# A second x tile transposed by DMA instead of on TensorE, in the opening of a linear-attention and token-MLP kernel

## The chip, the cores and the metric

The kernel runs on one core of a Trainium2 chip. The core has a matrix engine (TensorE, PE in the profile; its weight loads are listed as PEld), a vector engine (VectorE, DVE), a scalar engine (ScalarE, ACT), GpSimd (POOL), SyncE (SP), which here only issues DMA transfers, and 16 DMA engines that serve all queues. The metric is the device time of one execution in microseconds, as the median of several runs.

## The reference

Two branches read the same input x of 2048 rows (s) by 512 columns (d) and are mixed by a gate per row:

```
a = linear_attention(x)      # q,k,v = x @ wqkv, 32 heads of 16
    pq, pk = phi(q), phi(k)              # phi(t) = (t+1 if t>0 else exp(t)) + 1e-6
    kv = pk^T v ; z = sum over s of pk   # per head
    o = (pq kv) / (pq z + 1e-6) ; a = o @ wo
b = token_mlp(x)             # mixes along s, not along d
    h = layernorm(x)
    u = gelu(h^T @ w1 + b1)              # w1: 2048 x 1792
    b = (u @ w2 + b2)^T                  # w2: 1792 x 2048
g = sigmoid(sum over d of x * gate_w)
out = g * a + (1 - g) * b
```

All inputs are in bf16.

## The kernel before, in words

The 2048 rows are 16 tiles of 128 rows. Two copies of x are kept on chip: `xs` in its natural layout (row on the partition) and `xT` with the columns on the partition. k = x Wk needs `xT` as weights and `wk_sb` (Wk, four chunks of 128 x 512) as the moving operand. The kernel writes the order of all work by hand: every engine runs its instructions in the order in which the program lists them.

**The opening.** SP and ACT both issue loads. SP loads x tile 0 (L136), x tile 1 (L138) and Wk chunk 3 (L140) as plain transfers, and then tiles 2, 3 and 4 straight into `xT`, each by a DMA transpose of its own (L141, L142, issued by `load_xT`, L131). Behind them SP goes on, from L157 on, with a transpose of tiles 5 and 6 together, plain x tiles 2 and 3, a transpose of tiles 7 to 9, plain x tiles 4 to 7, a transpose of 10 to 12, plain tiles 8 to 15, a transpose of 13 to 15, and then wq, w1, wv and wo. ACT issues Wk chunks 0 and 1 in one transfer (L137) and chunk 2 (L139), and then loads its function table (L189).

**Tiles 0 and 1** are not transposed by DMA. TensorE multiplies each 128 x 128 block of `xs` by an identity matrix (`transpose_part`, L194, into PSUM tiles `pt`), and DVE or ACT copies the result to `xT` (`copy_part`, L199). While TensorE has no data it runs six matmuls of 128 x 512 on constants (`warm_up`, L184 and L190, tile `wps`).

**The k loop.** For tile t, `k_part` issues four matmuls into one PSUM bank `kacc`, and `k_phi` turns the bank into `pk` (ACT: exp; DVE: min/add and max/add). From t = 4 on, `g_tile(t-4)` adds four matmuls `gacc` with `xs` tile t-4 as weights and `pk` tile t-4 as moving operand. So TensorE alternates: k of tile 4, g of tile 0, k of tile 5, g of tile 1, and so on. The first two tiles (`HEADS = 2`, L281 to L293) have an order of their own, in which the chunks of k of tiles 0 and 1 are interleaved with the transposes of tile 1, and the layernorm statistics (`ln_step`) of both come before the loop. In the loop, `ln_step(t-5)` starts with t = 7.

**Later stages**, which the change leaves alone: q blocks together with the first three blocks of the MLP's first product (`uacc`, L404), the rest of that product (L443), and one loop over output tiles (L482) with attention output (`aps`) and the MLP's second product (`yps`). `load_w2` (L432) brings each of four column chunks of w2 in two transfers, issued in the third stage.

Transfers issued by SP and ACT share eight completion semaphores in turn. A transfer that takes a semaphore again waits until the eighth transfer before it has landed.

Of the kernel before, what the change touches and what calls it, by code (L numbers as in the profile page):

```python
# [15 lines left out]
def kernel(  # L16
# [13 lines left out]
    nc = tc.nc  # L30
# [10 lines left out]
    ND = D // P  # L41
    NF = F // P
    SC = 512
# [25 lines left out]
    def bank(name, dtype=FP32):  # L69
        return ps.tile([P, SC], dtype, name=name, tag="bank")  # L70
# [38 lines left out]
    def mm(o, lhsT, rhs, start, stop, **kw):  # L109
        nc.tensor.matmul(o, lhsT=lhsT, rhs=rhs, start=start, stop=stop, **kw)  # L110
# [14 lines left out]
    def load_x(q, t0, n):  # L125
        q.dma_start(out=xs[:, t0 : t0 + n, :], in_=x_view[:, t0 : t0 + n, :])

    def load_wk(q, k, n):
        q.dma_start(out=wk_sb[:, k : k + n, :], in_=wqkv_view[:, k : k + n, D : 2 * D])

    def load_xT(t0, n):  # L131
        nc.sync.dma_start(
            out=xT[:, :, t0 * P : (t0 + n) * P], in_=X[t0 * P : (t0 + n) * P, :], transpose=True
        )

    load_x(nc.sync, 0, 1)  # L136
    load_wk(nc.scalar, 0, 2)  # L137
    load_x(nc.sync, 1, 1)  # L138
    load_wk(nc.scalar, 2, 1)  # L139
    load_wk(nc.sync, 3, 1)  # L140
    for t in (2, 3, 4):  # L141
        load_xT(t, 1)  # L142
    nc.vector.memset(ones_f[:], 1.0)
    nc.vector.memset(mhalf[:], -0.5)
    nc.gpsimd.memset(ident[:], 0.0)
# [29 lines left out]
    def load_small():  # L175
        nc.gpsimd.dma_start(out=brow[0:NF, :], in_=B_b1.rearrange("(f q) -> f q", q=P))
        nc.gpsimd.dma_start(out=brow[NF : NF + NT, :], in_=B_b2.rearrange("(f q) -> f q", q=P))
        nc.gpsimd.dma_start(
            out=gw_b[:], in_=gate_w.rearrange("(o d) -> o d", o=1).to_broadcast([P, D])
        )  # L180
# [3 lines left out]
    def warm_up(n, cols=SC):  # L184
        for _ in range(n):
            mm(wps[:, :cols], warm[:, 0:P], warm[:, :cols], True, True)

    act_warm = keep([P, 1], FP32, "act_warm")
    nc.scalar.activation(out=act_warm[:], in_=ones_f[:], func=ACT.Exp)  # L189
    warm_up(6)  # L190

    pts = {}

    def transpose_part(t, k0, k1):  # L194
        pt = pts[t, k0, k1] = bank("pt")
        for k in range(k0, k1):
            mm(pt[:, k * P : (k + 1) * P], xs[:, t, k * P : (k + 1) * P], ident[:], True, True)

    def copy_part(t, k0, k1, on_act):  # L199
        src = pts.pop((t, k0, k1))[:, k0 * P : k1 * P].rearrange("p (k s) -> p k s", k=k1 - k0)  # L200
        dst = xT[:, k0:k1, t * P : (t + 1) * P]
        if on_act:
            nc.scalar.activation(out=dst, in_=src, func=ACT.Copy)
        else:
            nc.vector.tensor_copy(out=dst, in_=src)  # L205

    def phi(dst, acc):
        e = work.tile([P, SC], BF16, name="e", tag="e", bufs=6)
        nc.scalar.activation(out=e[:], in_=acc[:], func=ACT.Exp)  # L209
        nc.vector.tensor_scalar(  # L210
            out=e[:], in0=e[:], scalar1=1.0, scalar2=PHI_EPS, op0=ALU.min, op1=ALU.add
        )
        nc.vector.scalar_tensor_tensor(  # L213
            out=dst, in0=acc[:], scalar=0.0, in1=e[:], op0=ALU.max, op1=ALU.add
        )
# [3 lines left out]
    def k_part(t, ks):  # L219
        if t not in kaccs:  # L220
            kaccs[t] = bank("kacc")
        for k in ks:
            mm(
                kaccs[t][:], xT[:, k, t * P : (t + 1) * P], wk_sb[:, k, :],
                k == 0, k == ND - 1,
            )

    def k_phi(t):
        phi(pk[:, t, :], kaccs.pop(t))

    def ln_stats(t):
        stats = work.tile([P, nc.vector.BN_STATS_DIM], FP32, name="stats", tag="stats", bufs=2)
        nc.vector.bn_stats(out=stats[:], in_=xs[:, t, :])  # L233
        nc.vector.bn_aggr(out=mv[:, t, :], in_=stats[:])  # L234

    def ln_rstd(g):
        s = slice(g * TPC, (g + 1) * TPC)
        nc.vector.tensor_scalar_add(out=veps[:, s], in0=mv[:, s, 1], scalar1=EPS)
        nc.gpsimd.tensor_tensor(out=rstd[:, s], in0=veps[:, s], in1=mhalf[:], op=ALU.pow)

    def ln_shift(g):
        s = slice(g * TPC, (g + 1) * TPC)
        nc.vector.scalar_tensor_tensor(  # L243
            out=nmr[:, s], in0=mv[:, s, 0], scalar=-1.0, in1=rstd[:, s],
            op0=ALU.mult, op1=ALU.mult,
        )

    def ln_apply(t):
        nc.scalar.activation(  # L249
            out=hs[:, t, :], in_=xs[:, t, :], func=ACT.Identity,  # L250
            scale=rstd[:, t : t + 1], bias=nmr[:, t : t + 1],
        )
# [3 lines left out]
    def g_tile(t):  # L256
        if not gacc:
            gacc.extend(bank("gacc") for _ in range(ND))
        for k in range(ND):
            mm(gacc[k][:], xs[:, t, k * P : (k + 1) * P], pk[:, t, :], t == 0, t == NT - 1)  # L260
# [15 lines left out]
    def ln_step(u):  # L276
        ln_stats(u)
        if u % TPC == TPC - 1:
            ln_rstd(u // TPC)

    HEADS = 2  # L281
    for t in range(HEADS):
        for k0, k1 in ((0, 1), (1, 2), (2, ND)):
            transpose_part(t, k0, k1)
            copy_part(t, k0, k1, (t, k0) in ((0, 2), (1, 1)))
        k_part(0, range(2) if t == 0 else (2,))
    k_part(1, range(2))
    k_part(0, (3,))
    k_phi(0)
    k_part(1, range(2, ND))  # L290
    k_phi(1)
    ln_step(0)
    ln_step(1)  # L293
    LAG = 4
    LN_LAG = 5
    APPLY = 10
    for t in range(HEADS, NT):
        k_part(t, range(ND))
        k_phi(t)
        if t >= LAG:  # L300
            g_tile(t - LAG)
        if t > LN_LAG + 1:
            ln_step(t - LN_LAG)
        if t == TPC - 1 + LN_LAG:
            load_small()
        if t >= APPLY:
            ln_apply(t - APPLY)
        if t in (TPC + LN_LAG, 2 * TPC + LN_LAG):
            ln_shift((t - LN_LAG) // TPC - 1)
# [122 lines left out]
    def load_w2(c):  # L432
        w = wpool.tile([P, NT, FB * P], BF16, name="w2c", tag="wc")
        w2c.append(w)
        for f0 in (0, NF // 2):
            f1 = f0 + NF // 2
            nc.sync.dma_start(
                out=w[:, f0:f1, :], in_=w2_view[:, f0:f1, c * SC : (c + 1) * SC]
            )
# [3 lines left out]
    for j in range(NB0, NF):  # L443
        c, jj = divmod(j, FB)
        i = j - NB0
        acc = bank("uacc")
        for t in range(NT):
            if i == 2 and t < BRIDGE:
                for q in range(0, P, Q32):
                    c0 = jj * P + q  # L450
                    mm(
                        acc[q : q + Q32, :], w1c[c][:, t, c0 : c0 + Q32], hs[:, t, :],
                        t == 0, False, tile_position=(0, q),
                    )
                if t == BRIDGE - 1:
                    w2_matmuls()
                continue
            mm(acc[:], w1c[c][:, t, jj * P : (jj + 1) * P], hs[:, t, :], t == 0, t == NT - 1)
        gelu(j, acc)
        if i == 1:  # L460
            kv_matmuls()
            z_column()
        if 2 <= i < 2 + ND:
            w2_copies(i - 2)
        if 2 <= i < 2 + NDB:
            den_block(*divmod(i - 2, ND))
        if 2 <= i < 2 + NT // 2:
            gate_sum(2 * i - 4)
            gate_sum(2 * i - 3)
        if jj == FB - 1 or j == NF - 1:  # L470
            load_w2(c)
# [10 lines left out]
    for t in range(NT):  # L482
        c, tl = divmod(t, TPC)
# [54 lines left out]
```

## Time and profile before

| | |
|---|---|
| median of 3 runs | 163.08 us (162.43 to 163.41) |
| the profiled execution, own time | 162.26 us |
| its span in the trace | 160.6 us |
| TensorE busy | 155.9 us (97%), 822 matmuls recorded, 836 weight loads |
| VectorE busy | 124.3 us (77%) |
| ScalarE busy | 72.7 us (45%) |
| mean DMA rate | 144 GB/s |

Times in the trace start with the span. The span leaves out what lies around the program, 162.26 - 160.6 = 1.7 us here. A matmul of 128 x 512 is listed with 379 ns, but one starts every 216 ns when nothing waits, since matmuls overlap; so busy time is a count of "has something in it", and the start times tell the rate. A few matmul records are missing (822 against 836), and each leaves an idle hole of some 53 ns in the busy time though TensorE worked there. For a DMA the trace has three things: the stretch in which its queue issues it, the packets on the DMA engines, and the time from the start of the issue to the landing.

### The profile page before, as it was taken

The numbers are of one execution on the slowest core, as the hardware profiler recorded it, in microseconds if no ns is written. First come the engines' busy times: TensorE is split into PE (matmuls) and PEld (weight loads), VectorE is DVE, ScalarE is ACT, GpSimd is POOL, SyncE is SP. The second block draws the span as 40 slices with busy tenths as digits, with TensorE's granted clock in tenths as the row PEclk, the third lists the DMA queues.
The fourth block names the chain that finished last, engine by engine and source line by source line (L and its number), as shares of the span: only waits on it lengthen the run. The fifth ranks groups of instructions, "written<-read, shape, count | busy, mean of one in ns | idle before, by whom it ended". The sixth has DMA issues, their size and how long they took to land.

```text
span 160.6 us, 2228 instructions
## 1 busy us (share of the span) xinstructions
PE 155.9 (97%) x822; PEld 72.5 (45%) x836; DVE 124.3 (77%) x274; ACT 72.7 (45%) x113; POOL 7.3 (5%) x17
## 2 busy tenths in 40 slices
PE   7999999999999999999999999999999999999993
PEld 2444444444444445444444444444444444444462
DVE  1599999769999998756999999676999999711122
ACT  3543486654978393059873320237333442111110
POOL 3000332002010000000000000000000000000000
PEclk9999999999999999999999999999999999999999
DMA  5699999999970007600930679401000001110001
GB/s 168 150 231 262 328 352 329 354 349 348 336 171 0 0 0 257 204 0 4 356 101 2 213 244 306 151 33 37 33 33 33 33 33 58 48 61 33 33 33 33
DMA packets 29929, 23.07 MB, mean 144 GB/s; under 512 B 8384, under 2 KB 29888, under 8 KB 29920
## 3 DMA queue, kind: packets, MB, share of 16 engines
q1 hardware_dynamic: 29104, 22.15, 45.2%
q10 hardware_dynamic: 704, 0.66, 1.2%
q0 software_dynamic: 112, 0.14, 0.4%
q8 instruction: 6, 0.10, 0.3%
q14 instruction: 3, 0.02, 0.0%
HBM read 19.01 MB, written 2.10 MB: 131 GB/s over the span
## 4 chain that ended last, share of the span: by engine, by line
PE 84%; DVE 13%; issue 1%; ACT 0%
PE yps L110 30%; PE uacc L110 24%; PE kacc L110 9%; PE gacc L110 9%; PE aps L110 9%; DVE pqT L213 6%; DVE zacc L274 3%; DVE stats L233 2%; DVE e L210 2%; PE wps L110 2%; PE qacc L110 1%; DVE mv L234 1%; ACT e L209 0%; PE kvps L110 0%; PE w2ps L110 0%
## 5 line engine op out<-in xcount | busy, mean ns | idle before, releaser
L110 PE MATMUL uacc<-hs,w1c 128*128 128x512 bf16 (+1 forms) x227 | 50.8, 379 | 0.4 <-issue 0.2
L110 PE MATMUL yps<-uT,w2c 128*128 128x512 bf16 (+2 forms) x247 | 50.8, 355 | 0.3
L110 PEld LDWEIGHTS <-w2c 128*128 128x128 bf16 x252 | 23.6, 98 | 25.2
L110 PEld LDWEIGHTS <-w1c 128*128 128x128 bf16 (+1 forms) x233 | 21.8, 98 | 26.0 <-issue 0.2
L488 ACT ACTIVATE a_sc<-aps,c,gg 128x512 f32<-128x512 f32 x16 | 12.4, 775 | 31.2 <-PE aps L110 15.5
L501 DVE SCALAR_TENSOR_TENSOR ot<-yps,c,a_sc 128x512 bf16<-128x512 f32 (+2 forms) x18 | 12.3, 688 | 15.3 <-PE yps L110 11.7
L322 ACT ACTIVATE uT<-uacc,bcol 128x512 bf16<-128x512 f32 x14 | 9.3, 686 | 17.5 <-PE uacc L110 17.4
L110 PE MATMUL qacc<-xT,wq_sb 128*128 128x512 bf16 x64 | 16.4, 379 | 0.1
L110 PE MATMUL aps<-W2sb,pqT 128*128 128x512 bf16 x63 | 16.4, 379 | 0.1
L110 PE MATMUL kacc<-wk_sb,xT 128*128 128x512 bf16 x63 | 15.9, 379 | 0.2 <-DVE xT L205 0.2
L387 DVE STREAM_TRANSPOSE zT<-pz 128x512 f32<-128x512 f32 x16 | 11.3, 705 | 6.0 <-ACT pz L386 6.0
L110 PE MATMUL gacc<-pk,xs 128*128 128x512 bf16 x63 | 15.7, 379 | 0.1
L249 ACT ACTIVATE hs<-xs,nmr,rstd 128x512 bf16<-128x512 bf16 x16 | 12.8, 805 | 2.3 <-DVE nmr L243 2.3
L209 ACT ACTIVATE e<-kacc 128x512 bf16<-128x512 f32 x16 | 9.4, 594 | 9.7 <-PE kacc L110 8.5
L386 ACT ACTIVATE pz<-pqT,zcol 128x512 f32<-128x512 bf16 x16 | 11.4, 715 | 4.8 <-DVE ot L501 4.7
L209 ACT ACTIVATE e<-qacc 128x512 bf16<-128x512 f32 x16 | 9.5, 594 | 7.7 <-PE qacc L110 7.7
L396 DVE STREAM_TRANSPOSE rex<-rd 128x512 bf16<-128x512 bf16 x16 | 11.4, 711 | 0.6
L213 DVE SCALAR_TENSOR_TENSOR pqT<-qacc,e 128x512 bf16<-128x512 f32 x16 | 11.1, 692 | 0.6
L213 DVE SCALAR_TENSOR_TENSOR pk<-kacc,e 128x512 bf16<-128x512 f32 x16 | 11.1, 692 | 0.6
L389 DVE TENSOR_REDUCE den<-zT 128x32 f32<-128x512 f32 x16 | 11.0, 686 | 0.6
L210 DVE TENSOR_SCALAR e<-e 128x512 bf16<-128x512 bf16 x32 | 9.0, 282 | 2.5 <-ACT e L209 2.5
L233 DVE BATCH_NORM_STATS2 stats<-xs 128x6 f32<-128x512 bf16 x16 | 10.9, 683 | 0.0
(58 smaller groups left out, 96.2 us busy)
## 6 DMA issues: line engine op xcount, KB each, us to landing
w2c<-in_B_w_dram SPq DMA_DIRECT2D x8, 896.0 KB, 5.7
w1c<-in_B_w_dram SPq DMA_DIRECT2D x3, 2048.0 KB, 14.0
out_dram<-ot SPq DMA_DIRECT2D x13, 128.0 KB, 1.7
xs<-in_A_x_dram SPq DMA_DIRECT2D x1, 1024.0 KB, 6.6
w1c<-in_B_w_dram SPq DMA_DIRECT2D x1, 1024.0 KB, 15.3
xs<-in_A_x_dram SPq DMA_DIRECT2D x1, 512.0 KB, 5.0
wq_sb<-in_A_wqkv_dram SPq DMA_DIRECT2D x1, 512.0 KB, 5.6
wv_sb<-in_A_wqkv_dram SPq DMA_DIRECT2D x1, 512.0 KB, 12.3
```

Of the source, the lines that this page charges most:

```text
L110: nc.tensor.matmul(o, lhsT=lhsT, rhs=rhs, start=start, stop=stop, **kw)
L209: nc.scalar.activation(out=e[:], in_=acc[:], func=ACT.Exp)
L210: nc.vector.tensor_scalar(out=e[:], in0=e[:], scalar1=1.0, scalar2=PHI_EPS, op0=ALU.min, op1=ALU.add)
L213: nc.vector.scalar_tensor_tensor(out=dst, in0=acc[:], scalar=0.0, in1=e[:], op0=ALU.max, op1=ALU.add)
L233: nc.vector.bn_stats(out=stats[:], in_=xs[:, t, :])
L249: nc.scalar.activation(out=hs[:, t, :], in_=xs[:, t, :], func=ACT.Identity, scale=rstd[:, t : t + 1], bias=nmr[:, t : t + 1],)
L386: nc.scalar.activation(out=pz[:], in_=seg, func=ACT.Copy, scale=zcol[:, j : j + 1])
L387: nc.vector.transpose(out=zT[:], in_=pz[:])
L389: nc.vector.tensor_reduce(out=den[:], in_=zT[:].rearrange("p (a d) -> p a d", d=HEAD), op=ALU.add, axis=AX.X)
L396: nc.vector.transpose(out=rex[:].rearrange("p (a d) -> p a d", d=HEAD), in_=rd[:].unsqueeze(2).to_broadcast([P, SC // HEAD, HEAD]),)
L488: nc.scalar.activation(out=a_sc[:], in_=aps[:], func=ACT.Identity, scale=gg[:, t : t + 1], bias=c2[:, t : t + 1],)
L501: nc.vector.scalar_tensor_tensor(out=ot[:, :W], in0=yps[:, :W], scalar=c1[:, t : t + 1], in1=a_sc[:, cs], op0=ALU.mult, op1=ALU.add,)
```

## The change

Tile 1 of x is no longer transposed on TensorE. SP issues a DMA transpose for it right behind the plain load of tile 0, and the plain load of tile 1 moves behind the transposes of tiles 1 to 4. All of Wk is issued by ACT, in three transfers: chunk 0, chunk 1, and chunks 2 and 3 together. The sixth warm-up matmul has 256 columns instead of 512. `HEADS` is 1: only tile 0 has its TensorE transposes and copies, its four k matmuls follow in one go, and tile 1 is the first of the loop. `ln_step(1)` moves from before the loop to t = 6. The first chunk of w2 comes in one transfer instead of two.

```diff
     load_x(nc.sync, 0, 1)
-    load_wk(nc.scalar, 0, 2)
+    load_wk(nc.scalar, 0, 1)
+    load_wk(nc.scalar, 1, 1)
+    load_wk(nc.scalar, 2, 2)
+    for t in (1, 2, 3, 4):
+        load_xT(t, 1)
     load_x(nc.sync, 1, 1)
-    load_wk(nc.scalar, 2, 1)
-    load_wk(nc.sync, 3, 1)
-    for t in (2, 3, 4):
-        load_xT(t, 1)
...
-    warm_up(6)
+    warm_up(5)
+    warm_up(1, SC // 2)
...
-    HEADS = 2
-    for t in range(HEADS):
-        for k0, k1 in ((0, 1), (1, 2), (2, ND)):
-            transpose_part(t, k0, k1)
-            copy_part(t, k0, k1, (t, k0) in ((0, 2), (1, 1)))
-        k_part(0, range(2) if t == 0 else (2,))
-    k_part(1, range(2))
-    k_part(0, (3,))
+    HEADS = 1
+    for k0, k1 in ((0, 1), (1, 2), (2, ND)):
+        transpose_part(0, k0, k1)
+        copy_part(0, k0, k1, k0 == 2)
+    k_part(0, range(ND))
     k_phi(0)
-    k_part(1, range(2, ND))
-    k_phi(1)
     ln_step(0)
-    ln_step(1)
...
-        if t > LN_LAG + 1:
+        if t > LN_LAG:
             ln_step(t - LN_LAG)
...
-        for f0 in (0, NF // 2):
-            f1 = f0 + NF // 2
+        n = NF if c == 0 else NF // 2
+        for f0 in range(0, NF, n):
+            f1 = f0 + n
```

## The prediction

> **What bounds the kernel now.** I read the page first, then the busy time by stretches, then the opening on SP and TensorE instruction by instruction, with each DMA's time to landing.
>
> The page, and the busy time by stretches (columns: length of the stretch, PE busy and count, clock, DMA share, GB/s):
>
> ```profile
> span 160.6 us, 2228 instructions
> PE 155.9 (97%) x822; PEld 72.5 (45%) x836; DVE 124.3 (77%) x274; ACT 72.7 (45%) x113; POOL 7.3 (5%) x17
> PE 84%; DVE 13%; issue 1%; ACT 0%
> ...
> 3.36:4.06 0.70, 0.53 (x5) 1.00 1.10 377
> 4.06:6.20 2.14, 2.14 (x13) 1.00 0.69 167
> 6.20:9.65 3.45, 3.45 (x18) 1.00 0.68 153
> 9.65:157.40 147.75, 146.91 (x782) 1.00 0.47 145
> ```
>
> TensorE is the bound and has no slack behind 9.65 us: 0.84 us of idle time in 147.75, of which the 14 missing records explain 14 x 0.053 = 0.74. A microsecond that TensorE loses in the opening is lost at the end, and one won there is won, unless a later load then comes too late. The 13% of the chain on DVE lie between 34 and 55 us, where TensorE is just as full; that part starts from a TensorE result, so it moves with TensorE.
>
> The opening, on SP (start, length of the issue) and, below, the same five transposes' time from start of issue to landing:
>
> ```profile
> 1.27 0.41 SPq L126 DMA_DIRECT2D xs<-in_A_x_dram  x1
> 1.73 0.42 SPq L129 DMA_DIRECT2D wk_sb<-in_A_wqkv_dram  x1
> 2.20 1.30 SPq L132 DMA_TRANSPOSE xT<-in_A_x_dram  x1
> 3.54 1.26 SPq L132 DMA_TRANSPOSE xT<-in_A_x_dram  x1
> 4.84 1.27 SPq L132 DMA_TRANSPOSE xT<-in_A_x_dram  x1
> 6.16 1.30 SPq L132 DMA_TRANSPOSE xT<-in_A_x_dram  x1
> 8.13 1.42 SPq L132 DMA_TRANSPOSE xT<-in_A_x_dram  x1
> ```
>
> ```profile
> xT<-in_A_x_dram SPq DMA_TRANSPOSE x1, 3.5
> ...
> xT<-in_A_x_dram SPq DMA_TRANSPOSE x1, 2.8
> ...
> xT<-in_A_x_dram SPq DMA_TRANSPOSE x1, 2.7
> ...
> xT<-in_A_x_dram SPq DMA_TRANSPOSE x1, 3.1
> ...
> xT<-in_A_x_dram SPq DMA_TRANSPOSE x1, 4.0
> ```
>
> These are tiles 2, 3, 4, then 5 with 6, then 7 to 9. SP is busy issuing without a break: a transpose holds it for 1.26 to 1.42 us whether it carries one tile or three, a plain load for 0.41. Landings: tile 2 at 5.7, tile 3 at 6.3, tile 4 at 7.5, tiles 5 and 6 at 6.16 + 3.1 = 9.3, tiles 7 to 9 at 12.1.
>
> TensorE:
>
> ```profile
> 2.93 0.63 PE L110 MATMUL wps<-const-bfloat16-1.0 128*128 128x512 bf16 x1
> 3.36 0.53 PE L110 MATMUL pt<-ident,xs 128*128 128x128 bf16 x4
> 4.06 0.60 PE L110 MATMUL kacc<-wk_sb,xT 128*128 128x512 bf16 x2 [0.17 <-DVE xT L205]
> ...
> 9.43 0.74 PEld L110 LDWEIGHTS <-xT 128*128 128x128 bf16 x4
> 9.65 1.03 PE L110 MATMUL kacc<-wk_sb,xT 128*128 128x512 bf16 x4
> ```
>
> The last two lines are k of tile 5. Its weight load starts at 9.43; its data came at 9.3. So the opening is a race between SP's issue line and TensorE, and at tile 5 SP wins by under 0.2 us.
>
> **The change part by part.**
>
> *TensorE, head.* The sixth warm-up matmul starts at 2.93 and holds TensorE for 0.43 (cold rate, five starts in a row 0.43 apart); with half the columns until 3.15. x tile 0 lands at 0.81 + 2.3 = 3.1 and its weight load starts at 3.19 already, so the transposes start at about 3.24 instead of 3.36: 0.12 won. The four transposes of tile 1 (0.055 each, starts 4.50 to 4.67) go: 0.22. The stall of 0.17 before 5.11 for tile 1's copy goes too. In sum 0.5 on paper.
>
> *What takes the place of those stalls.* k of tile 0 now runs without a break, so its third matmul would come at 3.94 + 2 x 0.22 = 4.4. It needs Wk chunks 2 and 3, issued third on ACT: 0.81 + 0.46 + 0.49 and two small gaps = 1.8. Wk transfers landed 3.1 and 3.3 after the start of their issue, so these land at 4.9 to 5.1. The DMA engines are full there (share 1.10 above), and tile 1's transposed rows are now among the traffic, so I take 5.0. From 5.05 six matmuls follow (two of tile 0, four of tile 1, whose own data, issued at 1.25, land at 1.25 + 3.5 = 4.8 by the row of the first transpose): k of tile 2 starts at 5.05 + 6 x 0.216 = 6.35, against 6.20 before. The bounds are 6.2 and 6.4. The head's 0.5 is eaten by the wait for Wk.
>
> *SP's line.* It loses Wk chunk 3 (0.42 and a gap of 0.05) and gains one transpose (1.30 and 0.04); plain tile 1 only moves behind. Starts: tile 1 at 1.25, tile 2 at 2.6 (before 2.20), tile 3 at 3.9 (3.54), tile 4 at 5.2 (4.84), plain tile 1 at 6.5, tiles 5 and 6 at 6.98 (before 6.16). Everything that SP issues from there on is 0.82 us later. Tile 4 lands at 5.2 + 2.7 = 7.9; TensorE comes for it at 6.35 + 8 x 0.216 = 8.08, just in time. TensorE could start k of tile 5 at 8.08 + 8 x 0.216 = 9.81. Tiles 5 and 6 land at 6.98 + 3.1 = 10.09, so it starts at 10.14: 0.49 us later than 9.65. This is the term that counts. Bounds for the time to landing: 2.7 (one tile, quiet engines), which gives 9.7, so that TensorE's own 9.81 decides (+0.15); and 4.0 (three tiles right behind a plain load, as tiles 5 and 6 now are behind plain tile 1), which gives 10.99, a start at 11.04, +1.39. I take 3.1: the same transfer of the same size, and the plain load ahead of it has 128 KB, not the 256 of that row.
>
> *Who is late next.* Tiles 7 to 9 land at 12.14 + 0.82 = 12.96; k of tile 7 is due at 13.10 + 0.49 = 13.6. Plain tiles 4 to 7 landed at 14.6 for a weight load at 15.48: 15.4 against 15.97. Later loads had over 1 us. So the 0.49 is paid once and not again.
>
> *Hidden or free.* ACT's third DMA issue puts its table load (1.28) and first activation back by 0.49, to 3.8; its copy for tile 0 is due then, and the wait for Wk covers 0.5 of it. DVE loses three copies of tile 1 and does the statistics of tile 1 later, at t = 6; it idles 1.0 us between 28.0 and 32.3, and no TensorE matmul waited for it in the k loop. One w2 transfer instead of two is issued at about 60 us for a use at 96.
>
> [...] The rows say that issuing a transpose costs SP 1.30 us of the 2.7 to 3.5 until it lands. [...] I go by the rows. The trace also shows the matmul rate change: starts 0.43 apart until 3.36, 0.055 apart for 128 columns from 4.50 on. [...]
>
> *Sum.* Head and tail net into one start time: k of tile 5 at 10.14, +0.49. Span 160.6 + 0.5 = 161.1; the profiled execution 162.26 + 0.5 = 162.75. That execution is 0.82 below the median of the runs shown (163.08), so I forecast 163.08 + 0.5 = 163.6, which is +0.3%. A difference of 0.5% (0.82 us) is about what a measurement of this kernel can tell from none.
>
> **The rivals.**
>
> 1. *Slower than 0.5%: the two-tile transpose lands late.* Place: tiles 5 and 6, now right behind a plain load and behind one more transpose. For it: the row with 4.0. Against it: the DMA share in 6.20 to 9.65 is only 0.68, so the engines are not what it waits for. It decides from a landing after 10.42 (10.42 + 0.05 - 9.65 = 0.82); at the row's 4.0 the time is 163.08 + 1.39 = 164.5.
> 2. *Hidden or a small gain.* Wk chunks 2 and 3 land by 4.4 and the transposes issue or land faster than in these rows, so that TensorE keeps its 0.5. Then k of tile 2 starts at 5.7; tile 4 must land by 7.4 and tile 5 by 9.1, a whole 1.0 earlier than 10.09. Best case 163.08 - 0.5 = 162.6, with TensorE alone (+0.15) 163.2. Against it: five equal issue times in a row.
> 3. *The clock rises later.* With 0.21 us less activity and a new wait from 4.4 to 5.0, the first k matmuls could run at 0.43 instead of 0.216 apart. The cold stretch before was 0.85 to 4.06, 3.2 us; a second one would cost half, 1.6, less the two waits that it fills (0.6 and 0.3): +0.7 on the forecast, 164.3. For it: only that the rate depends on time at all.
>
> **How the numbers follow.** Forecast (+0.15 to +0.8, own range 163.2 to 163.9) 0.50; rival 1 0.27; rival 2 0.16; rival 3 0.07. The range runs from a small gain with the scatter of the runs, 162.7, to rival 1 at its row, 164.5. The forecast lies within 0.5% but for its upper end (0.85 of it), rival 1 is slower in nine of ten, rival 2 faster by over 0.5% only with scatter (a quarter), rival 3 mostly slower. Slower: 0.07 + 0.24 + 0.06 = 0.37; faster 0.07, with room for scatter; same 0.56.
>
> **What the profile of after would show.** Right: SP's transposes 1.3 us apart, the one of tiles 5 and 6 starting at 7.0; an idle gap of TensorE before k of tile 0's third matmul that ends with Wk's landing near 5.0; another of 0.3 us before k of tile 5, ended by `xT`'s DMA near 10.1; nothing behind it. Wrong: no gap at tile 5, or further gaps at tiles 7 or 10, or k matmuls 0.43 us apart after 4 us.

## The result, and the profile after

The changed kernel is slower: 165.81 us at the median of 12 runs (163.66 to 167.22), against 162.72 us (162.36 to 163.41) of the kernel before in 12 runs. The ratio is 1.0139 (95% interval 1.011 to 1.0168), that is 2.3 us on 162.72. The two medians lie 3.1 us apart. That ratio leaves out the five longest of the 12 runs; the profiled execution, with 166.99 us, is one of these, and why the runs spread over 3.6 us is part of the explanation below.

The page of the profiled execution, and the chain of waits in the opening in order of time (start, length):

```profile
span 165.1 us, 2231 instructions
PE 159.9 (97%) x832; PEld 72.9 (44%) x832; DVE 123.9 (75%) x272; ACT 72.5 (44%) x112; POOL 7.3 (4%) x17
```

```profile
1.74 4.77 DMA wk_sb<-in_A_wqkv_dram
6.51 0.04 issue
6.55 6.96 PE kacc L110 x18
13.51 0.86 PE gacc L110 x4
```

The span grew by 4.5 us, and TensorE's share is 97% as before: the page alone hides the loss. The chain shows it. Wk chunks 2 and 3, issued by ACT at 1.74, land 4.77 us later, at 6.51. Then 18 k matmuls take 6.96 us; at 0.216 us apart they would take 3.9.

TensorE in the opening, and the same by stretches (length, PE busy and count, PEld, DVE, ACT, POOL, clock, DMA share, GB/s):

```profile
3.58 0.61 PE L110 MATMUL pt<-ident,xs 128*128 128x128 bf16 x4 [0.23 <-DMA xs<-in_A_x_dram]
4.25 1.03 PE L110 MATMUL kacc<-wk_sb,xT 128*128 128x512 bf16 x2
6.55 6.96 PE L110 MATMUL kacc<-wk_sb,xT 128*128 128x512 bf16 x18 [1.26 <-DMA wk_sb<-in_A_wqkv_dram]
13.35 1.03 PE L110 MATMUL gacc<-pk,xs 128*128 128x512 bf16 x4
```

```profile
3.58:6.50 2.92, 1.64 (x6) 0.70 (x7) 0.49 (x2) 0.52 (x2) 0.00 (x0) 1.00 1.18 180
6.50:12.49 5.99, 5.94 (x15) 2.08 (x15) 3.45 (x8) 1.79 (x3) 0.00 (x0) 1.00 0.94 191
12.49:14.50 2.01, 2.01 (x11) 0.95 (x10) 1.32 (x4) 1.20 (x2) 0.00 (x0) 1.00 1.13 311
14.50:161.00 146.50, 146.50 (x777) 67.27 (x776) 117.34 (x255) 67.64 (x104) 5.90 (x7) 1.00 0.45 139
```

The clock column says 1.00 throughout, and that is a trap: the trace has no clock record before 12.49 in this execution (and before 3.65 in that of the kernel before), and a stretch without a record reads as 1.00. The distance of the matmuls is what tells. At this rate each matmul has a weight load that starts with it (from 6.55 on within 2 ns), and these are listed one by one:

```profile
11.20 0.15 PEld L110 LDWEIGHTS <-xT 128*128 128x128 bf16 x1 [0.28 <-issue]
11.62 0.15 PEld L110 LDWEIGHTS <-xT 128*128 128x128 bf16 x1 [0.28 <-issue]
12.05 0.15 PEld L110 LDWEIGHTS <-xT 128*128 128x128 bf16 x1 [0.28 <-issue]
12.47 0.54 PEld L110 LDWEIGHTS <-xT 128*128 128x128 bf16 x3 [0.28 <-issue]
```

From 6.93 to 12.47 the k matmuls start 0.43 us apart, which is half the rate; from 12.70 on they start 0.216 apart. From 14.5 on TensorE is never idle: the whole loss lies in the opening.

The sum: k of tile 5 starts at 14.2 here and at 9.65 before, 4.55 later, and the span is 4.5 longer. Of this, 1.65 is the wait for Wk (the third k matmul of tile 0 at 6.55, then 22 matmuls at 0.216 give 11.3), and 14 matmuls at 0.21 too much are the other 2.95. This is the account of one of the longest executions.

### The profile page after: what moved, and what is told of

The parts are those of the page before. It is cut to its first block, busy times and chain, and to the rows that moved or that the text cites. A ratio compares the mean times of both kernels' runs of the same rounds, so it can differ in the third digit from the quotient of the medians.

```text
span 165.1 us, 2231 instructions
## 1 busy us (share of the span) xinstructions
PE 159.9 (97%) x832; PEld 72.9 (44%) x832; DVE 123.9 (75%) x272; ACT 72.5 (44%) x112; POOL 7.3 (4%) x17
## 4 chain that ended last, share of the span: by engine, by line
PE 94%; DMA 3%; ACTq 1%; DVE 0%; issue 0%
PE uacc L110 29%; PE yps L110 29%; PE kacc L110 10%; PE aps L110 8%; PE qacc L110 8%; PE gacc L110 8%; DMA wk_sb<-in_A_wqkv_dram 3%; ACTq L129 1%; PE kvps L110 0%; PE w2ps L110 0%; DVE ot L497 0%; PE pt L323 0%
## 5 line engine op out<-in xcount | busy, mean ns | idle before, releaser
L110 PE MATMUL uacc<-hs,w1c 128*128 128x512 bf16 (+1 forms) x233 | 51.5, 379 | 0.0
L110 PE MATMUL kacc<-wk_sb,xT 128*128 128x512 bf16 x64 | 19.3, 441 | 1.3 <-DMA wk_sb<-in_A_wqkv_dram 1.3
L382 DVE STREAM_TRANSPOSE zT<-pz 128x512 f32<-128x512 f32 x16 | 11.3, 705 | 6.0 <-ACT pz L381 6.0
L110 PEld LDWEIGHTS <-xT 128*128 128x128 bf16 x64 | 7.0, 110 | 11.6 <-issue 5.3
```

The source lines that it names most:

```text
L382: nc.vector.transpose(out=zT[:], in_=pz[:])
```

## The experiments

They ask three things: what the late Wk costs and what the slow clock costs, what made the clock slow, and what made Wk late. The "mixed queues" theory in the first expectations is mine of that moment: transposes on SP's queue and plain transfers on ACT's queue slow each other. The "window" of the clock in the expectations of 2 and 4 is a supposition of mine; the records that bear on it are in experiment 3.

### 1. Wk chunks 2 and 3 on SP, ahead of the transposes

```diff
-    load_wk(nc.scalar, 2, 2)
+    load_wk(nc.sync, 2, 2)
     for t in (1, 2, 3, 4):
         load_xT(t, 1)
```

> The changed kernel, but Wk chunks 2 and 3 are issued by SP, between x tile 0 and the transpose of tile 1, and not by ACT. Theory (mixed queues: packets of a transpose on SP's queue and plain packets on ACT's queue slow each other while both are in flight): the Wk packets of chunks 2 and 3 are back near 46 ns each, they land at 4.6 to 5.0 instead of 6.5, TensorE waits for them 0.5 us at most, the clock rises before 7 us. What is left is SP's longer line: tiles 5 and 6 start at 7.6 and land near 11.0, so k of tile 5 starts 1.4 later than in the kernel before: 164.1. Rival (the engines are simply full in the opening): Wk still lands after 6, and the time stays above 165.3.

Measured: 163.84 us, ratio 1.0085 (1.0054 to 1.0116). The packets of chunks 2 and 3 took 46 to 50 ns; the chunks landed at 5.4, not at 4.6 to 5.0. The second and third k matmul, which waited for chunk 1 and for these, started 0.66 and 0.64 us after the one before, where 0.43 is the half rate: waits of 0.2 us each. In the profiled execution the clock was still at half rate until 9.07, and the clock part of the expectation failed there. Tiles 5 and 6 landed at 10.94, as expected. So where chunks 2 and 3 are issued is worth about 0.5% of the 1.4%; the two intervals just touch, and that of experiment 6, up to 1.0093, lies clear of the changed kernel's. The late clock came here with much smaller waits; how long a wait it takes was not measured.

### 2. The wait for Wk filled with matmuls

```diff
-    k_part(0, range(ND))
+    k_part(0, range(2))
+    warm_up(4)
+    k_part(0, range(2, ND))
```

> The changed kernel with four more matmuls of 128x512 on constants between the second and the third k matmul of tile 0, that is in the time in which TensorE waits for Wk. Theory (the idle wait keeps the TensorE clock at half rate for one window more): Wk still lands at 6.5, but k matmuls start 0.216 apart from there on; k of tile 5 starts at 6.55 + 22 x 0.216 = 11.3, 1.65 later than before, and the time is 164.4 with a smaller spread of runs. Rival (the clock has nothing to do with the wait, or the loss is all in the loads): 165.8 as the changed kernel.

Measured: 164.37 us (163.42 to 165.72), ratio 1.0111 (1.0076 to 1.0147). TensorE of this kernel:

```profile
5.03 1.91 PE L110 MATMUL wps<-const-bfloat16-1.0 128*128 128x512 bf16 x4
6.74 4.23 PE L110 MATMUL kacc<-wk_sb,xT 128*128 128x512 bf16 x18
10.81 1.03 PE L110 MATMUL gacc<-pk,xs 128*128 128x512 bf16 x4
```

Wk still landed late (1.73 + 4.6 = 6.3), but with work in the wait the 18 k matmuls take 4.23 us instead of 6.96. k of tile 5 starts at 11.67 (expected 11.3; the last filler matmul held k back until 0.4 after Wk had come). Work that computes nothing makes the kernel faster at the median than the changed one without it, though the two intervals overlap. The spread shrank less than I expected: 2.3 us in 9 runs against 3.6 in 12.

### 3. The sixth warm-up matmul at full length again

```diff
-    warm_up(5)
-    warm_up(1, SC // 2)
+    warm_up(6)
```

> The changed kernel with the sixth warm-up matmul at its full 512 columns again. Theory (the wait for Wk is what keeps the clock down): no visible difference, 165.0 to 166.5, k matmuls 0.43 apart until after 8 us in most executions. Rival (the 0.21 us less of warm-up is the cause): the clock is full from 4.5 us on and the time falls to 164.5 or less.

Measured: 165.75 us in four runs, ratio 1.0142 (1.007 to 1.0214): no difference that four runs can show. One run is at 164.1, the other three at 165.7 to 166.1, and the profiled one lost its clock with the full warm-up too, so the shorter warm-up is not needed for the loss. This execution also has clock records early enough to show how the clock moves. By stretches (length, PE busy and count, clock, DMA share, GB/s):

```profile
3.88:7.29 3.41, 1.30 (x8) 1.00 1.17 174
7.29:10.70 3.41, 3.41 (x10) 0.50 0.76 181
10.70:20.00 9.30, 9.30 (x44) 1.00 1.15 278
```

The clock was full from 3.88 on, TensorE was then busy for 1.30 of 3.41 us because of the wait for Wk, the clock fell to half for 3.41 us, TensorE was busy throughout, and the clock rose. In the kernel before and in the changed one the long record of full clock lasts 157.01 and 153.60 us, that is 46 and 45 times 3.413, and they differ by 3.41. The records fit a clock that is set window by window, 3.41 us long, from what TensorE did in the window before; this is my inference, above all from the one execution shown here. By these records it does not start with the kernel: the record of full clock begins at 3.65 in the kernel before, at 10.70 here behind the half one, and at 12.49 in the changed kernel, and whole windows of 3.413 taken off leave 0.24, 0.46 and 2.25 us. So the same wait could cost a different amount in each run. This fits the spread of the changed kernel; in the unprofiled runs the clock's phase wasn't seen. For the changed kernel, stepping back from 12.49 puts the edges of the windows at 9.08, 5.66 and 2.25, so the wait for Wk, from 5.29 to 6.55, lies in two of them. That would be why the clock rose only at the end of the third; it is an estimate from the 3.41 us, since no record lies there.

### 4. The clock alone: the kernel before with a short warm-up

```diff
-    warm_up(6)
+    warm_up(2)
```

> The kernel before with two warm-up matmuls instead of six; loads and everything else as they were. It prices the TensorE clock alone: TensorE idles from 1.7 to 3.2. Theory (the full clock is granted only after a window of activity, and the window has its own phase): the k matmuls start 0.43 apart until 6 to 9 us, 10 to 20 of them at 0.21 each; time 164.2 to 166. Rival (the rate rises with the time since the start, whatever TensorE does): 162.6.

Measured: 164.02 us (163.15 to 164.55), ratio 1.0072 (1.0045 to 1.0099). TensorE idled until x tile 0 came, with all loads as in the kernel before:

```profile
0.85 1.01 PE L110 MATMUL wps<-const-bfloat16-1.0 128*128 128x512 bf16 x2 [0.85 <-PEq L522]
3.15 0.61 PE L110 MATMUL pt<-ident,xs 128*128 128x128 bf16 x4 [1.29 <-DMA xs<-in_A_x_dram]
```

The k matmuls were 0.43 apart until 6.35 in the profiled execution, the shortest of the eight. The delayed clock by itself costs 0.7% here, 1.2 us, less than I expected (164.2 to 166).

### 5. All of Wk on ACT, in the kernel before

```diff
-    load_wk(nc.scalar, 0, 2)
-    load_x(nc.sync, 1, 1)
-    load_wk(nc.scalar, 2, 1)
-    load_wk(nc.sync, 3, 1)
+    load_wk(nc.scalar, 0, 1)
+    load_wk(nc.scalar, 1, 1)
+    load_wk(nc.scalar, 2, 2)
+    load_x(nc.sync, 1, 1)
```

> The kernel before with one part of the change alone: all of Wk on ACT in three transfers, so that SP's first transpose is issued at 1.73 instead of 2.20. Theory (mixed queues): the transpose of tile 2 meets Wk chunks 2 and 3 in the DMA engines, which land after 5.5, TensorE waits for chunk 3 and the time is 163.5 or more. Rival (issuing on ACT is harmless, it only frees SP): chunks 2 and 3 land by 5.1, every SP transfer comes 0.47 earlier, and the time is 162.7 or a little less.

Measured: 163.68 us, ratio 1.0077 (1.0039 to 1.0114). The landing of ACT's third transfer (KB, us from issue), and TensorE's wait for it:

```profile
wk_sb<-in_A_wqkv_dram ACTq DMA_DIRECT2D x1, 256.0 KB, 4.3
```

```profile
6.13 4.04 PE L110 MATMUL kacc<-wk_sb,xT 128*128 128x512 bf16 x18 [0.92 <-DMA wk_sb<-in_A_wqkv_dram]
```

This one part of the change, without a transpose more, makes Wk land at 6.08 and the kernel before slower by 0.8%. The prediction had counted it as a gain of 0.47 us on SP's line.

### 6. The rest of the change, with Wk as in the kernel before

```diff
-    load_wk(nc.scalar, 0, 1)
-    load_wk(nc.scalar, 1, 1)
-    load_wk(nc.scalar, 2, 2)
+    load_wk(nc.scalar, 0, 2)
+    load_wk(nc.scalar, 2, 1)
+    load_wk(nc.sync, 3, 1)
```

> The changed kernel with Wk loaded as in the kernel before: chunks 0 and 1 in one transfer and chunk 2 on ACT, chunk 3 on SP ahead of the transpose of tile 1, which is then issued at 1.73. Theory (mixed queues): the transposes meet only the last part of chunk 2; chunks 2 and 3 land at 4.8 to 5.6; tiles 5 and 6 start at 7.45 and land near 10.8, and the time is 163.5 to 164.5 with the clock in full from 4 to 9 us. Rival (a fourth transpose alone spoils the opening, wherever Wk comes from): Wk after 6, 165 or more.

Measured: 163.69 us (163.53 to 164.17), ratio 1.0069 (1.0046 to 1.0093), chunk 2 at 5.1, tiles 5 and 6 at 11.0. The clock part of the expectation failed here too: TensorE waited for chunk 2 and the matmuls were 0.43 apart until 6.12. It cost little, since TensorE came too early for tile 5 even so:

```profile
11.05 1.04 PE L110 MATMUL kacc<-wk_sb,xT 128*128 128x512 bf16 x4 [0.54 <-DMA xT<-in_A_x_dram]
```

### 7. Both faults of the opening taken out

Wk chunks 2 and 3 on SP as in 1, the full warm-up, and one matmul on constants in each of the two waits that are left:

```diff
+    load_wk(nc.sync, 2, 2)
...
+    warm_up(6)
...
+    k_part(0, range(1))
+    warm_up(1)
+    k_part(0, range(1, 2))
+    warm_up(1)
+    k_part(0, range(2, ND))
```

> The changed kernel with Wk chunks 2 and 3 on SP ahead of the transposes, the full sixth warm-up matmul and one matmul on constants in each of the two waits for Wk, so that TensorE is never idle for long. Theory (with the two faults of the opening gone, SP's longer issue line is what is left): the k matmuls start 0.216 apart before 6 us, TensorE could start k of tile 5 at 10.3 and waits for the transpose of tiles 5 and 6, which lands near 10.9; it starts near 11.0, 1.3 later than before; time 163.7 to 164.0. Rival (SP's line is hidden): no idle time before k of tile 5, time 163.2 or less.

Measured: 163.59 us (163.42 to 163.70 in five runs), ratio 1.0052 (1.0026 to 1.0078).

```profile
9.35 1.03 PE L110 MATMUL gacc<-pk,xs 128*128 128x512 bf16 x4
10.94 1.04 PE L110 MATMUL kacc<-wk_sb,xT 128*128 128x512 bf16 x4 [0.57 <-DMA xT<-in_A_x_dram]
```

Here the matmuls start 0.22 us apart from 5.00 on, the spread is 0.3 us, and what is left is the term of the prediction: TensorE is done with g of tile 0 and waits for the transpose of tiles 5 and 6, which lands at 10.90. k of tile 5 starts 1.29 later than before. SP's line is real; 0.47 of it is here the Wk transfer that went back to SP.

### 8. Is it the transposes? The first one issued later

The kernel of 5, with x tile 2 as a third plain load on SP ahead of the transposes:

```diff
     load_x(nc.sync, 1, 1)
+    load_x(nc.sync, 2, 1)
     for t in (2, 3, 4):
...
-    load_x(nc.sync, 2, 2)
+    load_x(nc.sync, 3, 1)
```

> The kernel before with all of Wk on ACT in three transfers, as in the run just before, but with one more plain load on SP ahead of the transposes (x tile 2, taken out of the later load of tiles 2 and 3), so that the first transpose is issued at 2.1 to 2.2 again and its packets come behind a third plain load. Theory (a transpose on SP's queue and plain packets on ACT's queue slow each other): the packets of Wk chunks 2 and 3 meet plain packets only, they land by 5.2 and not at 6.1, and the time is 162.4 to 162.9. Rival (it is the 256 KB transfer, or ACT's third one, that is slow): they land after 5.8, 163.3 or more.

Measured: 164.97 us in four runs, ratio 1.0127 (1.0072 to 1.0183). Wk chunks 2 and 3 landed at 6.58 and the third plain load of SP at 6.37. Wk was not earlier but later. Nor was it ACT's transfer alone; SP's third plain load, issued at 1.75, was as slow:

```profile
xs<-in_A_x_dram SPq DMA_DIRECT2D x1, 128.0 KB, 4.6
```

The mixed queues theory in the form that I had given it falls, and the rival holds as far as it goes: ACT's third transfer, or its 256 KB, is slow.

### 9. No transposes at all

In these kernels the transposition is left out: each transpose is replaced by plain transfers of the same rows in the same 256-byte pieces, so k and q are formed from the wrong elements. Only Wk's landing is read, from one execution each. First the changed kernel so altered (f1), then the kernel of 5 so altered, with SP kept quiet from 2 to 5 us by two small loads, the second of which waits for the first (f2):

```diff
-        nc.sync.dma_start(
-            out=xT[:, :, t0 * P : (t0 + n) * P], in_=X[t0 * P : (t0 + n) * P, :], transpose=True
-        )
+        for t in range(t0, t0 + n):
+            nc.sync.dma_start(
+                out=xT[:, :, t * P : (t + 1) * P],
+                in_=x_view[:, t, :].rearrange("p (k s) -> p k s", k=ND),
+            )
...
+    pause = keep([P, P], BF16, "pause")      # second kernel only
+    for _ in range(2):
+        nc.sync.dma_start(out=pause[:], in_=X[0:P, 0:P])
```

> The changed kernel with every DMA transpose replaced by plain transfers of the same rows in the same 256-byte pieces, one for each tile, so the transposition itself is left out and k and q are formed from rows in the wrong place. Only Wk's landing is looked at. Theory C (it takes transposes in flight beside Wk): chunks 2 and 3 land by 5.4, with packets near 46 ns, though SP issues plain tiles 1 to 4 every 0.45 us beside them. Theories A and B (three transfers, or 512 KB, on ACT's queue are slow by themselves): they land after 5.8.

> The kernel before with all of Wk on ACT in three transfers, with the transposes replaced in the same way (transposition left out), and with two loads of 32 KB on SP behind x tile 1, the second of which waits for the first, so that SP brings nothing else until about 4 us. Only Wk's landing is looked at. Theories A and B (ACT's queue by itself): chunks 2 and 3 land after 5.8 though hardly anything else is in flight. Theory C (transposes): they land by 4.8.

Theories A, B and C are these: A, a third transfer on ACT's queue is slow; B, 512 KB on ACT's queue are slow in whatever pieces; C, it takes transposes. Measured: chunks 2 and 3 were issued at 1.72 and landed at 5.82 in f1 and at 5.76 in f2. The row of f1:

```profile
wk_sb<-in_A_wqkv_dram ACTq DMA_DIRECT2D x1, 256.0 KB, 4.1
```

That is at the bound that I had drawn for A and B (5.8), and far from that of C (5.4 and 4.8). So Wk is late without a single transpose, and in f2 with hardly anything beside it. With transposes in flight the same third transfer landed at 6.1 to 6.9 in five kernels, so they seem to add to it. In four of these, where a transpose was issued ahead of it or with it, its packets took 79 to 120 ns at the mean, against 48 in f2.

### 10. The third transfer, or the bytes?

The quiet kernel of 9, f2, with other cuts of Wk (g1, g2, g3):

```diff
 g1: +    load_wk(nc.scalar, 0, 2)
     +    load_wk(nc.scalar, 2, 2)
 g2: +    load_wk(nc.scalar, 0, 1)
     +    load_wk(nc.scalar, 1, 1)
     +    load_wk(nc.scalar, 2, 1)
     +    load_wk(nc.sync, 3, 1)
 g3: +    load_wk(nc.scalar, 0, 2)
     +    load_wk(nc.scalar, 2, 1)
     +    load_wk(nc.sync, 3, 1)
```

> The kernel before with SP kept quiet behind x tile 1 and the transposition left out, as in the run just before, and all of Wk on ACT in two transfers of 256 KB. Theory A (the third transfer on ACT's queue is slow): chunks 2 and 3 land by 5.0. Theory B (512 KB on ACT's queue are slow in whatever pieces): they land after 5.4.

> The same with chunks 0, 1 and 2 on ACT in three transfers of 128 KB and chunk 3 on SP. Theory A: chunk 2 lands after 5.2. Theory B: it lands by 4.8.

> The same with Wk loaded as in the kernel before: chunks 0 and 1 in one transfer and chunk 2 on ACT, chunk 3 on SP. Control: by both theories chunk 2 lands at 4.6 and chunk 3 at 5.0, as there. If they land later, the loads' order is not what counts.

The last transfer of ACT in f2, in g1, in g2 and in g3 (KB, us from issue to landing):

```profile
wk_sb<-in_A_wqkv_dram ACTq DMA_DIRECT2D x1, 256.0 KB, 4.0
```

```profile
wk_sb<-in_A_wqkv_dram ACTq DMA_DIRECT2D x1, 256.0 KB, 3.7
```

```profile
wk_sb<-in_A_wqkv_dram ACTq DMA_DIRECT2D x1, 128.0 KB, 3.9
```

```profile
wk_sb<-in_A_wqkv_dram ACTq DMA_DIRECT2D x1, 128.0 KB, 3.6
```

Issued at 1.72, 1.30, 1.72 and 1.29, they landed at 5.76, 4.96, 5.62 and 4.90. As two transfers of 256 KB the whole of Wk is there at 4.96; as three of 128 KB, ACT's third one comes at 5.62 though it has a quarter of Wk's bytes. So the bytes are not what counts, and of the two theories A stands. The control g3 landed chunk 2 at 4.90 and chunk 3 at 5.22, 0.3 and 0.2 later than in the kernel before.

A is smaller than the landings make it look. Three transfers instead of two on ACT land 0.80 later with 256 KB (f2 against g1) and 0.72 later with 128 KB (g2 against g3), and 0.42 of each is only the later issue: from issue to landing the third took 0.3 to 0.4 longer than the second. Nor is it shown that ACT's queue is the reason: in g2 chunk 3 on SP took 3.7 too, against 3.5 in g3. That what counts is the number of transfers on both queues together is a rival that no run here separates. How the slow transfer looks, in the stretch from 3.5 to 4.0 us, f2 and then g1:

```profile
3.50:4.00 0.50, 0.50 (x5) 0.34 (x4) 0.17 (x1) 0.20 (x1) 0.00 (x0) 1.00 0.64 196
```

```profile
3.50:4.00 0.50, 0.41 (x5) 0.22 (x3) 0.29 (x2) 0.05 (x1) 0.00 (x0) 1.00 1.07 371
```

The DMA engines of f2 stand at a share of 0.64 and 196 GB/s while 256 KB of Wk are still to be moved; those of g1 run at 371. Each packet of Wk took 46 ns there, in both, so the engines of f2 were short of packets, and not slow with them. The changed kernel is not like that: its engines stand at 1.18 from 3.58 to 6.50 (above), and its packets of chunks 2 and 3 took 120 ns.

### 11. ACT's table load ahead of the transfers

In the slow kernels so far ACT's function table load follows right behind the third issue. Here it and the first activation come ahead of the three transfers (g4):

```diff
+    nc.vector.memset(ones_f[:], 1.0)
+    act_warm = keep([P, 1], FP32, "act_warm")
+    nc.scalar.activation(out=act_warm[:], in_=ones_f[:], func=ACT.Exp)
     load_x(nc.sync, 0, 1)
     load_wk(nc.scalar, 0, 1)
```

> The kernel of f2 (SP quiet, transposition left out, Wk on ACT in three transfers of 128, 128 and 256 KB), with ACT's function table load and first activation ahead of the three transfers instead of behind them, so all three are issued some 1.5 us later. Looked at is the time from the third one's start of issue to its landing, 4.0 in f2. Theory T (the table load behind it holds the third transfer up): 3.4 or less. Theory A alone (a third transfer on ACT's queue is slow whatever follows): 3.8 or more.

Measured: the transfers were issued at 0.98, 1.39 and 1.87, beside the table load and not 1.5 later as I had thought, and the third took 3.8 from issue to landing. A table load behind it is not the cause.

What stays open is the mechanism: why the third transfer gets its packets late. Also not measured is the kernel with transposes and all of Wk on ACT in two transfers of 256 KB, which g1 suggests.

## Why the prediction was wrong

**The step that failed** is "What takes the place of those stalls". It gave Wk chunks 2 and 3 the times of the first two transfers (3.1 and 3.3) and took 5.0 for their landing. They landed at 6.51, 4.77 after their issue. The rows of the kernel before had only two transfers on ACT's queue, and I carried their times over to a third one. Experiments 5, 9 and 10 show that the third one is another case: in the quiet f2, without transposes, it landed at 5.76, which is about half of the 1.5 us by which 5.0 was missed. The other 0.7 came with the transposes beside it; f2 differs in more than that, so this split is an estimate. The bounds that I drew, 4.9 to 5.1, were bounds of the wrong rows: nothing in the trace spoke of a third transfer, and that called for a wider bound above. The same step had tile 1's transposed rows at 4.8, by the first transpose's 3.5 from issue to landing. They landed at 6.87:

```profile
xT<-in_A_x_dram SPq DMA_TRANSPOSE x1, 5.6
```

The wait for Wk hides this. By the prediction's own steps TensorE wanted these rows at 5.05 + 2 x 0.216 = 5.5; also in experiments 1, 5, 6 and 7 SP's first transpose landed at 5.55 to 6.47. So Wk alone on time would hardly have given the forecast.

**The clock.** Rival 3 is what happened on top, at a chance of 0.07. I gave it two triggers, the shorter warm-up and the new wait from 4.4 to 5.0; no row of the kernel before shows that either holds the clock back, so both were supposition. Experiment 3 found no effect of the first. The wait is the one, and it was longer, 1.26 us of idle time: in experiment 3, with a wait of 1.90, TensorE was busy for 1.30 of 3.41 us and the clock then stood at half for 3.41 us, and with the wait filled in experiment 2 the full rate was there at 7.10. Its size was wrong too: I priced it at +0.7 on the forecast, by one cold stretch of 3.2 us less the waits in it; in the profiled execution it was 2.95, since the clock rose only at 12.49. I took the wait at its forecast length there. The 2.95 are also more than one window at half rate costs, 3.41 / 2 = 1.7 us as an estimate from the record of experiment 3. The two risks were one: the late load made the late clock.

**The head.** The transposes of tile 0 were to start at 3.24 and started at 3.58, since x tile 0 landed at 3.54 and not at 3.1. The 0.12 of the shorter warm-up was no gain. In nine other kernels whose first transfer on ACT, issued with that of x tile 0, has 128 KB instead of 256, x tile 0 landed at 3.41 to 3.72; where it has 256, at 2.88 to 3.42. That this is the cause was not tested apart.

**SP's line** was right in kind, somewhat small in size. Its issues were predicted at 1.25, 2.6, 3.9, 5.2, 6.5 and 6.98, and came at 1.27, 2.62, 3.91, 5.22, 6.54 and 7.16. Tiles 5 and 6 were to land at 10.09 and landed at 10.58. In the changed kernel itself nobody waited for them, since TensorE came at 14.2; experiments 6 and 7 uncover the gap at tile 5 that the prediction described (0.54 and 0.57 of idle time before k of tile 5). The two experiments still have 0.47 more on SP, so the forecast of +0.49 for this term alone has no run of its own. That, as the prediction says, a transpose holds SP equally long with one tile or three is true of the opening alone: those of tiles 10 to 12 and 13 to 15 held it for 2.21 and 4.12 us in the kernel before already.

**What was right besides:** nothing is late behind tile 5, the copies, the statistics and the w2 transfer cost nothing, and the gain of 0.5 at the head is eaten by the wait for Wk. **Rival 1** (a late two-tile transpose) was not it, though its sign was; **rival 2** needed Wk by 4.4 and falls with it. That issuing a transpose takes SP 1.30 us, as the prediction read from the rows, held in the opening: it took 1.23 to 1.30 of the 2.7 to 5.6 us until they landed, and experiments 6 and 7 show TensorE waiting for SP's line. Issuing from ACT what SP had issued was no gain: experiment 5, which does that with chunk 3 of Wk, is 0.8% slower.

## What to carry to other kernels

A duration read from the first transfers on a queue (here 3.1 and 3.3 us) was no bound for one more transfer behind them (3.8 to 5.1): count the transfers on each queue in the opening, and where the change adds one, widen the bound upward. Where TensorE is being brought to its full rate, price a wait of a microsecond or more (1.26 us in the changed kernel, 1.90 in experiment 3) as two terms, the wait itself and, as an estimate from these two, one or two windows of 3.41 us at half rate behind it. And read the rate from the distance of the matmuls, not from the clock column, before the first clock record.

## What the runs showed of the hardware that was not expected

- The third transfer in a row on ACT's queue landed 3.8 to 4.1 us after its issue without transposes beside it (f1, f2, g2, g4) and 4.3 to 5.1 with them, where the first took 2.3 to 3.0 as 128 KB and the second 2.8 to 3.7; a second one behind a first of 256 KB took 3.3 to 3.8. In f2 the DMA engines were at a share of 0.64 from 3.5 to 4.0 us, during the third.
- In the changed kernel itself, where the transposes of tiles 1 and 2 met Wk, a packet of chunks 2 and 3 took 120 ns at the mean (46 ns for those of chunk 1).
- In experiment 3 the TensorE clock stood at half for 3.41 us, right behind 3.41 us in which TensorE was busy for 1.30. The long records of full clock in the kernel before and in the changed one, 157.01 and 153.60 us, are 46 and 45 times 3.413, and begin at 3.65 and 12.49.
- Issuing a DMA transpose of one or two tiles held SP for 1.23 to 1.31 us per instruction in all the kernels that have them, also where it took twice as long to land (5.6 us against 2.7).
